# Neighborhood attention on one core: which queues issue the last stores of the output

## The chip, the core and the metric

The kernel runs on one core of a Trainium2 chip. The core has four engines that compute: TensorE (PE; its weight loads are shown apart as PEld), VectorE (DVE), ScalarE (ACT) and GpSimd (POOL). A fifth, SyncE (SP), issues transfers only. ACT and POOL can issue transfers too, each in the order of its own instructions. The metric is the device time of one execution in microseconds (us). A profile is one such execution with every instruction and transfer recorded; its span goes from the first instruction of the program to the last.

## What is computed

The reference is dilated 7x7 neighborhood attention with dilation 2 over an image of 224 x 224 pixels with 192 channels, one head, in bfloat16. Every pixel attends to 49 pixels, whose window is moved inwards at the image's edges:

```python
qkv = x @ wqkv                                  # 192 -> 3 * 192
r0 = clip(ir - half, 0, H - 1 - (ks - 1) * dil) # ks, dil = 7, 2
c0 = clip(ic - half, 0, W - 1 - (ks - 1) * dil)
kn, vn = the 49 rows of k and v that (r0, c0) + dil * (0..6) name
logits = einsum('bnc,bnkc->bnk', q, kn) * 192 ** -0.5
o = einsum('bnk,bnkc->bnc', softmax(logits), vn) @ wo
```

## The kernel before

**Tiling.** With dilation 2, rows of one parity only meet rows of the same parity, and columns likewise. The image is so cut into row classes `rc` (0 and 1) and column classes `cc` (0 and 1), with 112 rows and columns in each class. A step is 16 rows of one row class: 7 row tiles `ti` by 2 classes make `NSTEP` = 14 steps. A step holds `NSLOT` = 14 slots `s`, each of 16 rows by 8 columns of queries, that is 128 partitions, for both column classes. Slots are worked on in pairs, `J.m` = 0 to 6 with `ab` = 0 and 1, so that `s = 2 * J.m + ab`; the whole run has `NP` = 98 pairs, counted by `J.k`, and `J.n` is the step.

**Stages of a pair.** `stage1` multiplies queries and keys into `s` (L497) and takes the row maximum (L499, VectorE). `stage1b` is the exponential on ScalarE (L507). `stage2` transposes the probabilities on TensorE and copies them out of PSUM (L526, L527; L518 and L519 for the last pair). `stage3` multiplies them with the values into `o_ps` (L536); a column of ones beside the values gives the softmax's sum, whose reciprocal is taken in L542. `stage4` scales the output by it: on VectorE in L559, or, in the second slot of the last three pairs, with two instructions on ScalarE (L557), one for each column class. Those are slots 9, 11 and 13 of the last step.

**Stores.** The scaled slot is stored at the end of `stage4`. The 16 rows of a tile are not always evenly spaced in the image; `_aff_runs` cuts them into evenly spaced runs. In the last step (row class 1, row tile 6) the runs are 13 rows and three single rows. The 13 rows leave in one long store per slot (`put`, L565): 104 partitions, each with one contiguous piece of 768 B, 78 KB. All 13 of these, for slots 1 to 13, are issued by SP. The single rows are not stored slot by slot: the last step's outputs stand side by side in one tile, a reused `xs`, and `SHORT = {7: 1, NSLOT - 1: 8}` lets one short store carry one row for a group of slots (L576): at slot 7 three stores for slots 1 to 7 (8 partitions by 7 pieces, 42 KB), and at slot 13 three stores for slots 8 to 13 (8 by 6 pieces, 36 KB). The first three are issued by POOL at once. The last three are put on the list `end_q` and issued by ACT at the very end (L743 and L744).

Slot 0 has its own store code, because its columns wrap: many small pieces, queued in `pool_q` and issued by POOL (L588), some of them after each pair and the rest at the end (`pool_do`, L742).

**Order.** Each engine runs its instructions in the order in which the program wrote them (`in_order`, L745). A store waits in its issuer's queue for its data. All other waits are inserted by the framework from the tiles that are read and written; among them, a store takes one of a small number of semaphores in turn, and waits until that semaphore's last store has landed. After the last instruction each engine has a closing DRAIN and a barrier, which the profile puts under L771: SP waits there for all stores, and POOL gathers the other engines.

```python
                elif nj >= 8:
                    put(nc.sync)
...
                        if s < NSLOT - 1:
                            row(nc.gpsimd)
                        else:
                            end_q.append(row)
...
    pool_do(len(pool_q))
    for it in end_q:
        it(nc.scalar)
```

Of the kernel before, what the change touches and what calls it, by code (L numbers as in the profile page):

```python
# [21 lines left out]
NSLOT = 14  # L22
# [18 lines left out]
def _aff_runs(vals):  # L41
    out = []
    i, n = 0, len(vals)
    while i < n:
        j = i
        step = 1
        if i + 1 < n and vals[i + 1] > vals[i]:
            step = vals[i + 1] - vals[i]
            j = i + 1
            while j + 1 < n and vals[j + 1] - vals[j] == step:  # L50
                j += 1
        out.append((i, j - i + 1, vals[i], step))
        i = j + 1
    return out


def _rows(rc, ti):

    return [_phys(rc, 16 * ti + j) for j in range(16)]
# [7 lines left out]
def _win(t, p0, pn, off, dims):  # L67
    a = t[:]
    ps = a.ap[0][0]
    return bass.AP(a.tensor, a.offset + p0 * ps + off, [[ps, pn]] + [list(d) for d in dims])  # L70
# [18 lines left out]
def in_order(tc):  # L89

    last = {}
    for i in tc.nc.cur_bb.bb.instructions:
        if i.engine in last:
            tc.add_manual_dep(i, last[i.engine], mybir.DependencyInfo(mybir.DependencyClass.NoSync, mybir.DependencyReason.DATA), reason="program order")
        last[i.engine] = i.name
# [3 lines left out]
def kernel(  # L99
# [7 lines left out]
    nc = tc.nc  # L107
# [432 lines left out]
    def stage4a(J, ab):  # L540
        J.rs[ab] = stat.tile([128, 2], F32, name="rs", tag="rs")
        nc.vector.reciprocal(out=J.rs[ab][:], in_=J.o_ps[ab][:, C:C + 2])  # L542
        return J.rs[ab]

    def stage4(J, ab):
        rc, ti, s, o_ps = J.rc, J.ti, 2 * J.m + ab, J.o_ps[ab]
        rs = J.rs.get(ab) or stage4a(J, ab)
        if s > 0 and J.n == NSTEP - 1:

            o_sb = _win(XS[0], 0, 128, 2 * C * s, [[C, 2], [1, C]])  # L550
        elif s > 0:
            o_sb = work.tile([128, 2, C], BF, name="o_sb", tag="o_sb", bufs=6)
        else:
            o_sb = work.tile([128, 2, C], BF, name="o_s0", tag="o_s0")
        if J.k >= NP - 3 and ab == 1:
            for cc in range(2):
                nc.scalar.mul(o_sb[:, cc, :], o_ps[:, 194 * cc:194 * cc + C], rs[:, cc:cc + 1])  # L557
        else:
            nc.vector.tensor_tensor(out=o_sb[:], in0=_win(o_ps, 0, 128, 0, [[194, 2], [1, C]]),  # L559
                                    in1=rs[:].unsqueeze(2).to_broadcast([128, 2, C]), op=ALU.mult)  # L560
        prow = _rows(rc, ti)
        if s > 0:
            for (j0, nj, r0, rstep) in _aff_runs(prow):
                def put(eng, j0=j0, nj=nj, r0=r0, rstep=rstep):
                    eng.dma_start(out=op[r0: r0 + (nj - 1) * rstep + 1: rstep, 8 * s - 3:8 * s + 5, :],  # L565
                                  in_=o_sb[8 * j0:8 * (j0 + nj)].rearrange("p t c -> p (t c)"))

                if J.n < NSTEP - 1:
                    put(nc.gpsimd if nj < 8 and s % 2 == 1 else nc.sync)
                elif nj >= 8:  # L570
                    put(nc.sync)
                elif s in SHORT:

                    for j in range(nj):
                        def row(eng, p=8 * (j0 + j), r=r0 + j * rstep, a=SHORT[s]):
                            eng.dma_start(out=op[r, 8 * a - 3:8 * s + 5, :].rearrange("(t i) c -> i t c", i=8),  # L576
                                          in_=_win(XS[0], p, 8, 2 * C * a, [[2 * C, s + 1 - a], [1, 2 * C]]))
# [4 lines that stand above are left out]
            return  # L582
        for h in range(2):
            for (j0, nj, r0, rstep) in _aff_runs(prow[8 * h:8 * h + 8]):
                for (cc, i0, n, mem, pair) in ((0, 0, 3, 1, 0), (0, 3, 5, 0, 0), (1, 6, 2, 1, 3), (1, 0, 3, 1, 109), (1, 3, 3, 0, 109)):
                    p = 64 * h + 8 * j0 + i0 * nj
                    dst = op[r0: r0 + (nj - 1) * rstep + 1: rstep, pair:pair + n, mem * C:(mem + 1) * C]
                    pool_q.append(lambda dst=dst, p=p, m=n * nj, cc=cc: nc.gpsimd.dma_start(out=dst.rearrange("j i c -> i j c"), in_=o_sb[p:p + m, cc, :]))  # L588
# [17 lines left out]
    end_q = []  # L606
    SHORT = {7: 1, NSLOT - 1: 8}

    def pool_do(n):
        for _ in range(min(n, len(pool_q))):  # L610
            pool_q.pop(0)()
# [35 lines left out]
    for k in range(NP + 2):  # L647
# [22 lines left out]
        if k >= 2:  # L670
            stage3(pairs[k - 2], 0)
            stage3(pairs[k - 2], 1)
            if k >= NP:
                stage4a(pairs[k - 2], 0)
                stage4a(pairs[k - 2], 1)
            stage4(pairs[k - 2], 0)
            if k == NP - 1:
                stage4a(pairs[k - 2], 1)
# [6 lines left out]
        if k >= 2:  # L685
            stage4(pairs[k - 2], 1)
# [53 lines left out]
            g_row(1, 6, 1, 13, pool, last[1:])  # L740
        pool_do(4)
    pool_do(len(pool_q))  # L742
    for it in end_q:  # L743
        it(nc.scalar)  # L744
    in_order(tc)  # L745


# [28 lines left out]
```

## Time and profile before

| | |
|---|---|
| three runs, us | 365.96, 362.02, 364.18 (median 364.18) |
| profiled execution, us | 360.51 |
| its span, us | 358.7 |
| granted TensorE clock, mean | 0.995 |
| last step's long stores by SP (L565) | 13 of 78 KB, issue 794 to 873 ns |
| short stores by POOL (L576) | 3 of 42 KB, 593 to 620 ns |
| short stores by ACT (L576) | 3 of 36 KB, 301 to 538 ns |
| slot 0's stores by POOL (L588) | 150, 557 to 602 ns |

The profile's page gives for the whole span each engine's busy share, then the chain of work that ended last. Times of issue are those in which the issuing engine is held by the store; the transfer itself goes on after it. The transfers of the three issuers show as three queues, of which q1 and q10 are called hardware dynamic and q0 software dynamic:

```profile
q1 hardware_dynamic: 130052, 56.32, 78.5%
q0 software_dynamic: 5280, 1.71, 2.7%
q10 hardware_dynamic: 2120, 1.54, 2.3%
```

The columns are packets, MB, and the time of the packets as a share of 16 DMA engines over the span. POOL's stores are those of q0. The landing of a store is the moment at which its semaphore has its last update.

### The profile page before, as it was taken

The page shows a single profiled execution, that of the slowest core. Times are in us where ns is not written, and L with a number is a line of the kernel's source. Part 1 is how long each engine was busy: PE and PEld are TensorE (multiplying, and loading weights), DVE is VectorE, ACT ScalarE, POOL GpSimd, SP SyncE. Part 2 cuts the span into 40 slices and gives each one's busy share as a digit, 9 for nine tenths or more (in the row PEclk, how much of TensorE's full clock was granted, in tenths as well). Part 3 has the DMA queues.
Part 4 walks back from the last instruction along what each step waited for, and adds up shares of the span by engine and source line. Part 5 has one row for each costly group of instructions (what it writes and reads, how often), then busy time and mean ns, then how long its engine had stood idle before and what let it go on. Part 6 is the DMA issues. An engine that isn't in the chain of part 4 may idle for free.

```text
span 358.7 us, 19454 instructions
## 1 busy us (share of the span) xinstructions
PE 333.6 (93%) x8120; PEld 307.1 (86%) x8120; DVE 314.2 (88%) x744; ACT 308.2 (86%) x824; POOL 282.6 (79%) x445
## 2 busy tenths in 40 slices
PE   4788888998999999999999999999999999999872
PEld 2777777997999999999989999999999999999762
DVE  8967987897898998989989999899998989989893
ACT  6354777997999999999999999999999989999893
POOL 8966799999896996959969699596996878374182
PEclk9999999999999999999999999999999999999998
DMA  9999876799968979889898997999989965635423
GB/s 191 214 189 182 161 168 160 152 206 154 209 158 201 189 177 184 185 187 195 182 191 178 203 194 170 188 196 187 193 182 187 179 143 123 142 98 116 107 68 90
DMA packets 137539, 60.79 MB, mean 169 GB/s; under 512 B 88578, under 2 KB 136927, under 8 KB 137452
## 3 DMA queue, kind: packets, MB, share of 16 engines
q1 hardware_dynamic: 130052, 56.32, 78.5%
q0 software_dynamic: 5280, 1.71, 2.7%
q10 hardware_dynamic: 2120, 1.54, 2.3%
q8 instruction: 63, 1.03, 1.2%
q14 instruction: 24, 0.20, 0.2%
HBM read 0.29 MB, written 19.27 MB: 55 GB/s over the span
## 4 chain that ended last, share of the span: by engine, by line
PE 74%; DVE 10%; POOL 7%; ACT 5%; issue 2%; DMA 1%; DVEq 0%; SPq 0%; POOLq 0%; ACTq 0%
PE pv L341 17%; PE s L497 16%; PE o_ps L536 15%; PE pg L421 11%; PE pt_ps L526 10%; PE pgh L421 6%; ACT p L507 3%; POOL out_dram L588 2%; POOL xs L170 2%; DVE xb L160 2%; DVE nmx L499 2%; DVE g L329 1%; POOL xb L160 1%; POOL g L456 1%; ACT pt_sb L527 1%
## 5 line engine op out<-in xcount | busy, mean ns | idle before, releaser
L507 ACT ACTIVATE p<-s,nmx 128x224 bf16<-128x224 f32 x392 | 150.1, 450 | 25.7 <-DVE nmx L499 24.2
L499 DVE TENSOR_REDUCE nmx<-s 128x2 f32<-128x392 f32 (+1 forms) x196 | 102.5, 565 | 18.2 <-PE s L497 17.5
L456 POOL COPY g<-gx 64x512 bf16<-64x512 bf16 (+1 forms) x110 | 62.1, 564 | 52.7 <-ACT gx L331 45.8
L341 PE MATMUL pv<-wp,xs 128*64 128x192 bf16 x1624 | 93.1, 250 | 10.8 <-DVE xs L366 3.6
L341 PEld LDWEIGHTS <-xs 128*64 128x64 bf16 x1624 | 79.0, 112 | 24.0 <-issue 8.5
L559 DVE TENSOR_TENSOR o_sb<-o_ps,rs 128x384 bf16<-128x384 f32 x169 | 94.2, 558 | 5.9
L331 ACT CAST vf<-pv 128x384 bf16<-128x384 f32 x193 | 87.8, 522 | 11.1 <-PE pv L341 11.1
L588 POOL DMA_DIRECT2D out_dram<-o_s x150 | 84.6, 571 | 9.0 <-DVE rs L542 7.8
L536 PE MATMUL o_ps<-vd,pt_sb 128*64 128x193 bf16 x784 | 81.6, 246 | 2.3 <-ACT pt_sb L527 2.1
L497 PE MATMUL s<-xa,g 128*64 128x196 bf16 (+7 forms) x990 | 82.3, 233 | 1.2 <-ACT p L507 0.3
L497 PE MATMUL s<-xb,g 128*64 128x196 bf16 (+7 forms) x990 | 82.0, 232 | 0.7 <-DVE g L329 0.4
L536 PE MATMUL o_ps<-vf,pt_sb 128*64 128x193 bf16 x784 | 81.6, 246 | 0.0
L497 PEld LDWEIGHTS <-g 128*64 128x64 bf16 x1980 | 77.8, 110 | 3.6 <-issue 2.0
L536 PEld LDWEIGHTS <-pt_sb 128*64 128x64 bf16 x1568 | 71.5, 109 | 3.8 <-ACT pt_sb L527 3.2
L527 DVE COPY pt_sb<-pt_ps 128x1024 bf16<-128x1024 bf16 x92 | 63.2, 687 | 6.0 <-PE pt_ps L526 0.8
L526 PE MATMUL pt_ps<-ident,p 128*64 128x128 bf16 x1552 | 63.7, 219 | 0.0
L526 PEld LDWEIGHTS <-p 128*64 128x64 bf16 x1552 | 57.1, 110 | 4.9
L331 ACT CAST g<-pg 128x512 bf16<-128x512 f32 (+4 forms) x136 | 57.6, 470 | 2.3 <-PE pg L421 2.3
L421 PEld LDWEIGHTS <-aw 128*64 128x64 bf16 x1320 | 54.7, 110 | 3.9 <-issue 0.6
L421 PE MATMUL pg<-xb,aw 128*64 128x512 bf16 (+9 forms) x440 | 54.1, 269 | 0.0
L421 PE MATMUL pg<-xa,aw 128*64 128x512 bf16 (+9 forms) x440 | 52.3, 270 | 0.0
L170 POOL COPY xs<-xa 128x896 bf16<-128x896 bf16 x50 | 45.2, 930 | 1.4
(73 smaller groups left out, 283.9 us busy)
## 6 DMA issues: line engine op xcount, KB each, us to landing
vd<-vf SPq DMA_DIRECT2D x49, 336.9 KB
out_dram<-o_sb SPq DMA_DIRECT2D x156, 96.0 KB
out_dram<-o_s POOLq DMA_DIRECT2D x78, 9.0 KB, 3.9
out_dram<-o_sb SPq DMA_DIRECT2D x13, 78.0 KB
out_dram<-xs SPq DMA_DIRECT2D x13, 78.0 KB
vd<-vf SPq DMA_DIRECT2D x2, 337.8 KB
vd<-vf ACTq DMA_DIRECT2D x2, 336.9 KB
xa<-in_x_dram SPq DMA_TRANSPOSE x28
```

The costliest lines, as they stand in the source:

```text
L331: nc.scalar.copy(out=out_, in_=in_)
L341: nc.tensor.matmul(pv[64 * h:64 * h + 64, cc * C:(cc + 1) * C], lhsT=at(k, h), rhs=WP[(cc, pas)][:], start=(pas == 0), stop=(pas == 1))
L421: nc.tensor.matmul(o, lhsT=l, rhs=r, start=(pas == 0), stop=(pas == 1))
L456: nc.gpsimd.tensor_copy(out=G[rc][cc][p:p + 64, 1, s0:s0 + ns, :], in_=gx[p:p + 64, 0:ns * 128].rearrange("p (s q) -> p s q", q=128))
L497: nc.tensor.matmul(o, lhsT=w, rhs=r, start=(pas == 0), stop=(pas == 1))
L499: nc.vector.tensor_reduce(out=nmx[:], in_=_win(s_ps, 0, 128, lo, [[256, 2], [16, 14], [1, 16 - lo]]), axis=AX.XY, op=ALU.max, negate=True)
L507: nc.scalar.activation(out=J.p[:, ab, cc, :, z:z + 112].rearrange("p q (r k) -> p q r k", k=8), in_=_win(s_ps, 0, 128, cc * 256, [[8, 2], ...
L526: nc.tensor.transpose(pt_ps[64 * h:64 * h + 64, 4 * ab + 2 * cc + q, :], J.p[:, ab, cc, q, 64 * h:64 * h + 64], ident[:])
L527: (nc.scalar.copy if J.n == NSTEP - 1 and J.m < 5 else nc.vector.tensor_copy)(out=J.pt[:], in_=pt_ps[:])
L536: nc.tensor.matmul(o_ps[64 * h:64 * h + 64, cc * 193:cc * 193 + 193], lhsT=J.pt[:, 4 * ab + 2 * cc + q, 64 * h:64 * h + 64], rhs=V[h][:, ( ...
L559: nc.vector.tensor_tensor(out=o_sb[:], in0=_win(o_ps, 0, 128, 0, [[194, 2], [1, C]]), in1=rs[:].unsqueeze(2).to_broadcast([128, 2, C]), op ...
L588: pool_q.append(lambda dst=dst, p=p, m=n * nj, cc=cc: nc.gpsimd.dma_start(out=dst.rearrange("j i c -> i j c"), in_=o_sb[p:p + m, cc, :]))
```

## The change

The long stores of two slots of the last step get another issuer: slot 11 (`NSLOT - 3`) goes to POOL and slot 13 (`NSLOT - 1`) to ACT. The three short stores of the last group, which ACT issued one after the other, are dealt out to SP, POOL and ACT. In the order of instructions this gives: SP has 11 long stores in place of 13, and one short store behind them; POOL has, behind the last of slot 0's stores, the long store of slot 11 and one short store; ACT has, behind its last scaling, the long store of slot 13 and one short store in place of three. What is stored, and where, is the same.

```diff
                 if J.n < NSTEP - 1:
                     put(nc.gpsimd if nj < 8 and s % 2 == 1 else nc.sync)
                 elif nj >= 8:
-                    put(nc.sync)
+
+                    put({NSLOT - 3: nc.gpsimd, NSLOT - 1: nc.scalar}.get(s, nc.sync))
                 elif s in SHORT:
...
     pool_do(len(pool_q))
-    for it in end_q:
-        it(nc.scalar)
+    for i, it in enumerate(end_q):
+        it((nc.sync, nc.gpsimd, nc.scalar)[i % 3])
     in_order(tc)
```

## The prediction

> **What bounds the kernel now.** I read the page first, then the last 6 us engine by engine, since the change touches only stores behind the last computation.
>
> ```profile
> span 358.7 us, 19454 instructions
> PE 333.6 (93%) x8120; PEld 307.1 (86%) x8120; DVE 314.2 (88%) x744; ACT 308.2 (86%) x824; POOL 282.6 (79%) x445
> PE 74%; DVE 10%; POOL 7%; ACT 5%; issue 2%; DMA 1%; DVEq 0%; SPq 0%; POOLq 0%; ACTq 0%
> ```
>
> Over the whole span TensorE sets the pace, and the edit leaves all of that as it is. The chain of waits, printed for its last stretch, ends like this (start, length, what):
>
> ```profile
> 353.33 0.03 ACTq L576
> 353.36 0.28 ACT xs L557
> ```
>
> The chain closes at 353.64 with ScalarE's last scaling, yet the span ends at 358.74: 5.1 us (1.4% of the span) hold only stores, their landings and the closing barrier. No edit of stores can gain more than a part of that. The timeline of those microseconds, each row asked for in a narrow window (start, length):
>
> ```profile
> 352.63 0.80 SPq L565 DMA_DIRECT2D out_dram<-xs  x1
> 353.52 0.81 SPq L565 DMA_DIRECT2D out_dram<-xs  x1
> 354.43 0.79 SPq L565 DMA_DIRECT2D out_dram<-xs  x1
> 355.32 0.81 SPq L565 DMA_DIRECT2D out_dram<-xs  x1
> ...
> 352.48 0.41 ACT L557 ACTIVATE xs<-o_ps,rs 128x192 bf16<-128x192 f32 x1
> 353.22 0.41 ACT L557 ACTIVATE xs<-o_ps,rs 128x192 bf16<-128x192 f32 x1
> 353.66 0.54 ACTq L576 DMA_DIRECT2D out_dram<-xs  x1
> 354.24 0.30 ACTq L576 DMA_DIRECT2D out_dram<-xs  x1
> 354.58 0.46 ACTq L576 DMA_DIRECT2D out_dram<-xs  x1
> ...
> 351.78 0.57 POOL L588 DMA_DIRECT2D out_dram<-o_s  x1
> ```
>
> SP's four rows are the long stores of slots 10, 11, 12 and 13, one every 0.90 us. Slot 11's data is ready at 352.90 and slot 13's at 353.64 (the ends of L557), but they are issued at 353.52 and 355.32. So slot 13 waits 1.68 us for its turn in SP's queue. Its landing is the last one: the semaphore records have it at 357.66, 2.34 us after its issue began, and SP's closing waits end on it (us in total, times, longest):
>
> ```profile
> SPq L771 <- DMA out_dram<-xs: 1.2, 2, 0.7
> ```
>
> From that landing to the span's end it is 1.08 us of semaphore steps. The last view is of the closing line, L771 (op, count, duration in ns min/median/max, first and last start):
>
> ```profile
> L771 SPq EVENT_SEMAPHORE  x12: 17/28/28, 356.2 to 358.7; - x12
> L771 POOLq EVENT_SEMAPHORE  x4: 17/17/17, 358.0 to 358.6; - x4
> L771 POOLq DRAIN  x3: 40/93/5003, 351.4 to 358.5; - x3
> L771 ACTq DRAIN  x2: 8/124/239, 355.1 to 358.2; - x2
> ```
>
> The reader is to see the 5003. POOL ends with a DRAIN that begins beside its last store (351.44), ends at 356.44, and stands ahead of the barrier step at 358.02 in which POOL gathers the other engines. Before the change it is covered for 1.58 us. The change gives POOL two later stores.
>
> **The change, part by part.** Nothing before 352.9 us moves: SP keeps its stores up to slot 10, POOL its list, and the computation does not depend on these stores.
>
> SP loses the long stores of slots 11 and 13 and gains one short store. Slot 12 (data ready at 353.32, the end of VectorE's last L559) takes slot 11's place at 353.52; the short store follows one pitch later, 354.42, and lasts 0.30 to 0.54 by ACT's rows, so SP is done at 354.87 instead of 356.13. By ACT's rows (issue starts 353.66, 354.24, 354.58; landings recorded at 355.77, 356.36, 356.87) a short store lands 2.1 to 2.3 us after its issue begins: 356.5 to 356.7.
>
> ACT swaps three short stores for the long one of slot 13 and one short. It is free at 353.66 as now. The long one costs ACT something between its own short rows (0.54) and SP's long rows (0.81); I take 0.81, being the same transfer. Short one at 354.51 to 354.97, landing at 356.8. ACT's three short issues ended at 355.04, so behind it ACT's drain (0.24) comes no later. The added wait on slot 13's data is on ACT's own work; nothing else is queued there.
>
> POOL gains the long store of slot 11 and a short one, behind its last L588 (free at 352.36). Slot 11 waits for ACT's 352.90 and starts at 352.95; the short one waits for ACT's 353.64 and starts at 353.69. The nearest rows of POOL are its 42 KB stores, L576 (0.62 a piece, landing after 2.6 to 2.7); the far one is the seven early L565 stores, up to 0.73 and landing after 2.9 to 5.3 while the DMA engines were nine tenths busy. In the last stretch they are about half busy, so I take L576: issue ends at 353.6 and 354.31, landings at 355.6 and 356.35. Behind these two waits on ACT stands nothing in POOL's queue but its drain, for which the closing barrier waits.
>
> Stores alone: the last landing goes from 357.66 to 356.8, a gain of 0.86 us. On this the Trainium skill speaks against the change: its page "DMA: Bandwidth & Descriptors", section "Issuing engines are not separate DMA queues", says that transfers from all issuers interleave on the same 16 DMA engines, and that issuing from several saves only issue time, usually small beside the transfer. The trace has issue at 0.90 us a store beside 1.5 us from issue's end to landing, so small is not the word here; by the page alone the term would be near zero.
>
> Now the drain. What ends it the trace does not say, so it is bounded by three anchors. After the end of POOL's last issue (352.36) it lasted 4.08 us: with the last issue ending at 354.31, that is 358.39. After the landing of that store (353.88) it lasted 2.56: 356.35 + 2.56 = 358.91. After its own start, which lay beside the last store, 5.00: 353.6 + 5.0 = 358.6. I take the middle, 358.6. POOL then gathers at 358.64, and the 0.73 from there to the end are as before (358.02 to 358.74): the span ends near 359.4, 0.6 us later than now. Lower bound: the drain follows nothing POOL issues, and the end is 356.8 + 1.08 = 357.9, a gain of 0.9. Upper bound: the short store lands after 5.3 us (359.0) and the drain 2.56 behind it (361.55), span end 362.3, a loss of 3.6.
>
> On the drain the skill's page "VectorE: DVE Perf Modes", section "The DRAIN you can't avoid", has boilerplate drains at about 12 ns on all engines; the row says 5003 ns on POOL behind its stores and 8 to 239 on ACT, so the trace disagrees for POOL. By the page the lower bound would be the result.
>
> **Rivals.**
> Forecast: POOL's drain takes the place of SP's queue, +0.4 to +0.9 us. For it: the drain is long only where POOL has just issued stores (5003 ns, against 40 and 93 in the two that follow). Against it: one instance only. Chance 0.55.
> Gain as written: the drain stays covered and the last landing sets the end, 357.9, gain 0.9 us. For it: nothing shows what the drain waits for. Chance 0.27.
> Shared engines: three issuers' packets mix, and the last landing stays near 357.6, about 0. Against it: the DMA engines' share between 354 and 357 is 0.53, 0.58 and 0.51, so there is room. Chance 0.08.
> Slower: the drain is POOL working off runs of its stores. The last six stores have 3 x 56 + 6 + 9 + 9 = 192 contiguous runs, begun at 348.80 and drained at 356.44, 40 ns a run; the two new ones have 13 x 8 + 6 x 8 = 152, 6.1 us more: drained at 362.5, the end at 363.3, a loss of 4.6 us (1.3%). It decides once a run costs over 10 ns, for 152 x 10 ns uses up the 1.58 us of cover. Against it: those stores had landed by 353.9, and copies of POOL that stand right behind bursts of stores earlier in the run took their usual 0.6 us. Chance 0.10.
> That the stores are not moved is no rival: the instruction order of the two kernels differs in exactly these rows on SP, ACT and POOL.
>
> **How the numbers follow.** The profiled execution took 360.51 us (span 358.74 and 1.77 around it); the median of the three runs is 364.18, and they spread over 3.9 us. The forecast gives 361.1 on the former, a ratio of 1.0017, so 364.8 on the median; the gain case gives 363.3, shared engines 364.2, the slower case 368.8. A median of three such runs wanders by some 1.3 us, so about 1.7 is added on either side: 361.6 from the gain case, 366.5 from the forecast, to which I add 0.5 for the late landings of the upper bound. Range 361.7 to 367.0; the slower case stays outside. About 1% (3.6 us) is what a measurement of this kernel can tell from no change. The forecast and the two small cases lie within it save for that wander (a few per cent on either side), and the slower case is mostly beyond: faster 0.04, same 0.84, slower 0.12.
>
> **What would show it.** SP's last issue near 354.4 with a short store, ACT's long store at 353.66, POOL's two at 352.95 and 353.69, and the last landing near 356.8: then the stores went as costed. POOL's DRAIN ending at 358.4 to 358.9, later than SP's last closing wait, and the span near 359.4: then the forecast holds. A drain ending before 357.2 makes it wrong towards the gain; one ending after 360 means that it grows with what POOL stores.

## The result, and the profile after

The changed kernel took 365.33 us (median of 10 runs, 362.55 to 366.71); the kernel before took 361.83 us (median of 10, 360.37 to 365.96). The ratio is 1.0059, 95% interval 1.0031 to 1.0087: slower, by less than 1%. The two medians alone would give 1.0097. Ratios leave out runs more than 1.5% above the fastest of their kernel (one of twelve and four of six in two of the experiments below). The profiled execution took 363.49 us, with this span:

```profile
span 361.7 us, 19456 instructions
```

Two different things stand in the 3.0 us between the two spans, and the first step is to part them. ScalarE's last scaling ended at 353.63 before and at 355.80 after. Up to there both kernels run the same instructions, and the distance between the two traces does not grow steadily: it comes in two jumps, 1.06 us near 224 us and 1.30 us near 268 us. This is the wait view of the changed kernel from 266 to 280 us (us in total, times, longest):

```profile
ACT vf L331 <- DMA vd<-vf: 1.6, 1, 1.6
DVE nmx L499 <- PE s L497: 1.3, 2, 1.1
```

ScalarE may not write new values into `vf` before an earlier copy out of it has landed. In this execution the copy was late; in the same stretch of the kernel before the first row is absent. The chain of waits has such a copy ahead of the first jump too, from 217.94 to 223.04. Nothing that was moved runs there.

The second thing is the end. From the last scaling to the end of the span it took 5.11 us before and 5.91 us after: 0.80 us more. The timeline after, in the order SP, ACT, POOL (start, length):

```profile
354.80 0.80 SPq L565 DMA_DIRECT2D out_dram<-xs  x1
355.69 0.81 SPq L565 DMA_DIRECT2D out_dram<-xs  x1
356.60 0.43 SPq L577 DMA_DIRECT2D out_dram<-xs  x1
...
355.39 0.41 ACT L557 ACTIVATE xs<-o_ps,rs 128x192 bf16<-128x192 f32 x1
355.83 1.51 ACTq L565 DMA_DIRECT2D out_dram<-xs  x1
357.44 0.32 ACTq L577 DMA_DIRECT2D out_dram<-xs  x1
...
355.36 0.59 POOL L565 DMA_DIRECT2D out_dram<-xs  x1 [0.85 <-ACT xs L557]
356.12 0.57 POOL L577 DMA_DIRECT2D out_dram<-xs  x1 [0.17 <-issue]
```

SP is done earlier, as meant: its last issue ends 1.22 us behind the last scaling, against 2.50 before. ACT's long store holds it for 1.51 us, where SP's take 0.80. The closing line and SP's waits:

```profile
L772 SPq EVENT_SEMAPHORE  x12: 17/28/28, 357.1 to 361.6; - x12
L772 POOLq EVENT_SEMAPHORE  x4: 17/17/17, 361.0 to 361.6; - x4
L772 POOLq DRAIN  x3: 40/93/4837, 356.1 to 361.4; - x3
L772 ACTq DRAIN  x2: 8/122/237, 357.8 to 361.2; - x2
```

```profile
SPq L772 <- DMA out_dram<-xs: 1.9, 3, 1.0
SPq L772 <- PEq L772: 1.9, 2, 1.4
```

POOL's long DRAIN begins at 356.10 and takes 4837 ns, so it ends at 360.94; POOL's first closing step stands at 361.0 right behind it. SP has had its last landing (3.56 us behind the last scaling) and its last drain by 359.69, and then waits 1.4 us more for the barrier; the name PE in that row is only the one whose signal the profile saw last. Before, the order was the other way round: POOL's drain was over 1.58 us ahead of the barrier step.

### The profile page after: what moved, and what is told of

The parts are those of the page before. It is cut to its first block, busy times and chain, and to the rows that moved or that the text cites. A ratio compares the mean times of both kernels' runs of the same rounds, so it can differ in the third digit from the quotient of the medians.

```text
span 361.7 us, 19456 instructions
## 1 busy us (share of the span) xinstructions
PE 333.2 (92%) x8120; PEld 306.7 (85%) x8120; DVE 314.4 (87%) x744; ACT 308.3 (85%) x824; POOL 282.9 (78%) x447
## 3 DMA queue, kind: packets, MB, share of 16 engines
q8 instruction: 63, 1.03, 1.2%
## 4 chain that ended last, share of the span: by engine, by line
PE 68%; DVE 10%; ACT 7%; POOL 7%; DMA 4%; issue 2%; DVEq 0%; POOLq 0%; ACTq 0%
PE pv L341 16%; PE s L497 15%; PE o_ps L536 14%; PE pg L421 10%; PE pt_ps L526 9%; PE pgh L421 5%; ACT p L507 5%; DMA vd<-vf 3%; DVE nmx L499 2%; POOL out_dram L589 2%; POOL xs L170 2%; DVE xb L160 2%; POOL xb L160 1%; DMA out_dram<-o_sb 1%; POOL g L456 1%
```

## The experiments

All of them are read by one clock, us behind the end of ScalarE's last scaling, since what comes ahead of that point differs from execution to execution in kernels that are equal there: it ended between 353.63 and 359.34 in the ten executions up to `pool_many`. Each number of this table comes from the instruction and semaphore records of one profiled execution. Five of the kernels ran once only, so their times are not compared: `pool_long_only` 361.29, `pool_short_only` 366.99, `late_copy` 368.21, `early35_sp` 388.60 and `late20_sp` 370.15 us.

| kernel | POOL's last store or copy ends | DRAIN ends | DRAIN behind it | last landing | end of span |
|---|---|---|---|---|---|
| before | -1.28 | 2.81 | 4.08 | 4.03 | 5.11 |
| same_as_before | -1.28 | 2.81 | 4.08 | 3.99 | 5.07 |
| after | 0.89 | 5.13 | 4.25 | 3.56 | 5.91 |
| after_again | 0.89 | 5.14 | 4.25 | 3.55 | 5.92 |
| slot10_pool | -0.14 | 4.02 | 4.17 | 3.75 | 4.89 |
| no_pool | -1.29 | 2.79 | 4.08 | 3.99 | 4.95 |
| pool_long_only | 0.15 | 4.32 | 4.17 | 3.93 | 5.10 |
| pool_short_only | 0.93 | 5.09 | 4.16 | 3.98 | 5.88 |
| late_copy | 2.54 | 6.64 | 4.10 | 3.99 | 7.42 |
| pool_many | 2.59 | 7.08 | 4.49 | 4.40 | 7.86 |
| early35_sp | -0.24 | 1.73 | 1.97 | 4.05 | 5.42 |
| late20_sp | -1.28 | 1.32 | 2.60 | 3.97 | 5.31 |
| slot0_sp | -1.45 | 0.87 | 2.33 | 4.00 | 5.15 |
| slot0_sp_after | 0.89 | 3.97 | 3.08 | 3.63 | 4.79 |

The theory: POOL's closing DRAIN follows POOL's last store and now ends last. Rivals: the moved stores cost time in the middle too; the drain grows with the runs that POOL stores; the drain does not depend on the stores at all.

**Two yardsticks.** `same_as_before` walks over a copy of the list and is otherwise the kernel before; `after_again` is the changed kernel.

> The kernel before under another name, as the yardstick of what two equal programs differ by. Both theories: ratio 1.000 within about 0.3%, and 5.1 us from the end of ScalarE's last scaling to the end of the span (5.11 in the profile before).

> The changed kernel once more. Theory 1, only the end of the run is different: 5.9 us from ScalarE's last scaling to the end (5.9 in the profile after, 5.1 before), so a ratio near 1.002, and the 2.2 us by which the scaling ended later in the profile after were chance (two stalls in the middle, near 224 and 268 us). Rival, the moved stores cost something in the middle too: ratio near 1.006 again, and the last scaling ends 1 us or more later than in the two profiles of the kernel before.

Measured: 0.9996 (0.9971 to 1.0022) for the one, 1.0013 (0.9986 to 1.0039) for the other, 12 runs each beside 35 of the kernel before. The end takes 5.92 us, within 0.01 of the first time, and the last scaling ended at 354.17, beside 353.63 and 354.38 in the two executions of the kernel before. So the end is what differs, and the 2.2 us in the middle did not come back. 0.80 us is 0.22% of the run, which lies in the second interval and below the first.

**One store of POOL at a time.** First the long store of slot 11 alone, then one short store alone:

```diff
-                    put(nc.sync)
+                    put({NSLOT - 3: nc.gpsimd}.get(s, nc.sync))
```

> The kernel before with slot 11's long store by POOL, nothing else moved. POOL's issue ends 0.1 us before ScalarE's last scaling does. If the drain follows POOL's last store: it ends 4.0 to 4.1 us behind the scaling, and the end takes 4.8 to 4.9 us, 0.2 to 0.3 less than before. If the drain costs time per contiguous run of the stores (40 ns each): 104 runs are 4.2 us more work, 8 us or more to the end.

```diff
-    for it in end_q:
-        it(nc.scalar)
+    for i, it in enumerate(end_q):
+        it((nc.scalar, nc.gpsimd, nc.scalar)[i % 3])
```

> The kernel before with one of the three last short stores by POOL, nothing else moved. SP's thirteen long stores are as before, so without POOL's drain the end takes 5.1 us. If the drain follows the last store: its issue ends 0.7 us behind the last scaling, the drain 4.8 to 4.9 behind it, and the end takes 5.6 to 5.7 us.

The short store alone gives the whole loss: 5.88 us, with SP's last landing at 3.98 as before. This is the closing drain of that kernel, 359.7 being 0.32 behind its last scaling:

```profile
L771 POOLq DRAIN  x3: 40/102/4778, 359.7 to 364.9; - x3
```

The long store alone, the 104 runs, is nearly free: 5.10 us. The drain is so no matter of runs (8 us or more was the price). It missed the 4.8 to 4.9 expected from the drain for two reasons that the records show. POOL began the store 0.30 us behind ScalarE's data, where 0.05 had been taken. And SP's slot 13, issued 0.89 us earlier than before, landed only 0.10 earlier: from issue to landing it took 3.13 us in place of 2.34. That second part is what the rival of shared engines would give; it stands on one execution, and the cause was not isolated.

**Does the drain wait for the store?** POOL gets a copy behind its last store that waits for ScalarE's last scaling; no store is moved, and the copy adds to no output.

```diff
     pool_do(len(pool_q))
+    pool(out=VD[0][:, 0:7, 0:2 * C], in_=_win(XS[0], 0, 128, 2 * C * 7, [[2 * C, 7], [1, 2 * C]]))
     for it in end_q:
```

> The kernel before with no store moved; POOL copies 128 x 2688 elements of the last outputs to a tile no longer used, behind its last store and behind ScalarE's last scaling (some 2.5 us), and so its DRAIN begins later than its last store. The copy adds to no output. If the drain waits for something of the last store (4.1 us behind its issue): it is over when the copy ends, and the end takes 5.1 us as before. If it is a piece of work of its own length, 4 to 5 us from when POOL gets to it: it ends 6.5 us or more behind the scaling, and the end takes 7.3 us or more.

POOL's timeline and its closing line in that kernel:

```profile
355.99 1.74 POOL L588 DMA_DIRECT2D out_dram<-o_s  x3
359.14 2.42 POOL L743 COPY vd<-xs 128x2688 bf16<-128x2688 bf16 x1 [1.42 <-ACT xs L557]
...
L772 POOLq DRAIN  x3: 40/102/6533, 359.1 to 366.2; - x3
```

The stores were issued by 357.73, and the copy ran to 361.56. The drain began beside the copy, at 359.13, and took 6533 ns, to 365.66: 4.10 us behind the end of the copy, 7.93 behind the last store. Had it waited for something of the store, it would have been over 0.3 us after the copy. So it follows POOL's last instruction, be it a store or a copy, and takes some 4 us of its own in this kernel. The forecast had the right length but tied it to the store. (In every run POOL issues stores, 25 at the least, so what the drain would take on a POOL without stores is not shown.)

**Five stores by POOL.** The long stores of slots 11 and 13 and the three short ones:

```diff
-                    put(nc.sync)
+                    put({NSLOT - 3: nc.gpsimd, NSLOT - 1: nc.gpsimd}.get(s, nc.sync))
...
+        it((nc.gpsimd, nc.gpsimd, nc.gpsimd)[i % 3])
```

> The kernel before with five of its last stores by POOL: the long ones of slots 11 and 13 and the three short ones, 352 contiguous runs. Issue at about 0.6 us each ends 2.4 us behind the last scaling. If the drain follows the last store at 4.1 to 4.3 us: the end takes 7.4 us, 2.3 more than before, ratio 1.006. If it grows with the runs or the number of stores, it takes longer than that behind the last issue: with 40 ns a run, 14 us more.

Ratio 1.0126 (1.0075 to 1.0178), with the end at 7.86 us. The 2.75 us more at the end are 0.76%, just inside that interval; the 1.006 expected is below it. The drain grew by 0.41 us over the kernel before for five stores; with one store it was 0.09 and 0.08, with two 0.17. That is 0.08 a store and far from 40 ns a run, which would be 14 us.

**Without POOL, and with POOL early.** In the first slot 13's long store goes to ACT and the short stores to SP, ACT and ACT, and slot 11's long store stays with SP; in the second slot 10's long store, whose data is ready 1.03 us ahead of the last scaling, is the only one moved.

```diff
-                    put(nc.sync)
+                    put({NSLOT - 1: nc.scalar}.get(s, nc.sync))
...
+        it((nc.sync, nc.scalar, nc.scalar)[i % 3])
```

> The change without POOL: the long store of slot 13 by ACT, slot 11's by SP as before, the three short ones by SP, ACT and ACT. POOL's drain is covered again by every theory. If SP and ACT issue independently (long store 0.8 us on ACT): last landing 3.6 us behind the last scaling, 4.9 us to the end. If the two share what makes their transfers (ACT's long store took 1.51 us beside SP's in the profile after): 5.1 to 5.3 us, no gain.

```diff
-                    put(nc.sync)
+                    put({NSLOT - 4: nc.gpsimd}.get(s, nc.sync))
```

> The kernel before with one edit: the long store of slot 10 is issued by POOL, all others as before. If POOL's closing DRAIN follows its last store (4.1 to 4.25 us behind the end of that issue in the two profiles), that issue ends 0.4 us before ScalarE's last scaling does, the drain ends 3.8 us behind the scaling, SP's last landing 3.5 behind it, and the whole end takes 4.65 us: 0.45 less than before, ratio 0.999. If a late store of POOL costs more than it saves in any case: over 5.1 us.

`no_pool`: ratio 1.0016 (0.9980 to 1.0051). ACT's rows there:

```profile
356.83 1.51 ACTq L565 DMA_DIRECT2D out_dram<-xs  x1
358.44 0.66 ACTq L576 DMA_DIRECT2D out_dram<-xs  x2
```

The long store holds ACT for 1.51 us again, and the last landing is at 3.99, no earlier than in `same_as_before`. That speaks for a shared resource: 416 + 144 = 560 runs are issued by SP and ACT in 3.3 to 3.5 us whichever of them issues (from slot 10's store on). ACT's short stores point the same way: one took 0.54 us beside a long store of SP (before, 353.66) and 0.32 us when SP was through (after, 357.44). The end at 4.95 is near the 4.9 of the other forecast and 0.12 below `same_as_before`, but not through an earlier landing: SP is through its closing waits sooner (4.13 for 4.25). It takes these waits one by one at 0.06 us each, and after the store that lands last one of them follows here, three in `same_as_before`. What is shared was not isolated: ACT's long store was never issued with SP idle.

`slot10_pool`: ratio 0.9992 (0.9967 to 1.0016). The end is 0.2 us shorter than in the two executions of the kernel before (4.89), not 0.45. SP's last landing came at 3.75, not 3.5, and SP was through its waits at 4.07. POOL's start is again 0.30 late, and the drain ends at 4.02, just ahead of that. It is the shortest end of those that leave the middle as it is, and too small a gain for the runs to show.

**What the drain works at.** Since it grew by 0.08 us a store, four kernels take stores from POOL: those of slot 0 in the first three steps, in the two steps before the last, and in all but the last step, the last also in the changed kernel.

```diff
-                    pool_q.append(lambda dst=dst, p=p, m=n * nj, cc=cc: nc.gpsimd.dma_start(out=dst.rearrange("j i c -> i j c"), in_=o_sb[p:p + m, cc, :]))
+                    pool_q.append(lambda dst=dst, p=p, m=n * nj, cc=cc, eng=nc.sync if J.n < 3 else nc.gpsimd: eng.dma_start(out=dst.rearrange("j i c -> i j c"), in_=o_sb[p:p + m, cc, :]))
```

> The kernel before with the 35 stores of slot 0 of the first three steps issued by SP: POOL issues 125 stores in place of 160. So far the closing DRAIN took 4.08, 4.17, 4.16, 4.25 and 4.49 us behind POOL's last issue with 160, 161, 161, 162 and 165 stores, and 4.10 behind a copy. Theory 1, it works through all stores of POOL's run at 0.08 us each: 1.2 us behind the last issue. Theory 2, only the stores since some earlier point late in the run count (some 49): 4.08 again. Theory 3, a fixed piece of work: 4.08 again. The end takes 5.1 us in all three.

> The kernel before with the 20 stores of slot 0 of the two steps before the last issued by SP: POOL issues 140 stores. Theories 1 and 2 (0.08 us a store): the drain takes 2.4 us behind POOL's last issue. Theory 3, a fixed piece of work with little for each store: about 4.08. The end takes 5.1 us in all three.

> The kernel before with all stores of slot 0 by SP except those of the last step: POOL issues 25 stores. Theories 1 and 2: the drain takes at most 2.1 us. Theory 3: about 4.1. The end takes 5.1 us; the ratio is 1.00 if SP's queue has room in the middle of the run, more if stores and loads wait there for the 135 that are added.

> The changed kernel with the same move: POOL issues 27 stores. Theories 1 and 2: the drain ends 0.89 + 2.25 = 3.1 us behind ScalarE's last scaling, is covered by the last landing at 3.55, and the end takes 4.65 us, 0.45 less than in the kernel before. Theory 3: the end takes 5.8 us as in the changed kernel.

No theory holds. Only `late20_sp` comes near a price of the first two (2.60 us for 2.4); `early35_sp` came at 1.97 for 1.2 or 4.08. A fixed piece of work falls: 1.97 and 2.60 us are well below 4.08. The number of POOL's stores falls as the only measure: 125 stores give 1.97, 25 give 2.33, 27 give 3.08. What sets the length is open; near the 160 stores of this kernel it is 4.1 us and 0.08 more for each. (The ends of the first two, 5.42 and 5.31, are above the 5.1 expected. Their drains were long over; SP was through its waits 0.2 us later. In `late20_sp` seven of SP's waits follow the store that lands last, where three do in the kernel before; in `early35_sp` the cause is open.)

But the pair answers the question of the change. Where the drain is short, the same edit gains at the end: 4.79 against 5.15 us. The two closing drains:

```profile
L771 POOLq DRAIN  x3: 40/93/3254, 429.7 to 437.0; - x3
```

```profile
L772 POOLq DRAIN  x3: 40/102/3672, 439.4 to 443.6; - x3
```

The first is that of `slot0_sp`, the second of `slot0_sp_after`, where it ends 3.97 behind the scaling, level with SP's last wait (3.96). This gain of 0.36 us is read from one execution of each, and whole runs don't show it: the medians of six runs are 445.44 and 445.45 us. As kernels both are of no use, at ratios of 1.2077 (1.2019 to 1.2134) and 1.2248 (1.2200 to 1.2296). The wait view of `slot0_sp` over the whole span points to the reason:

```profile
POOL g L456 <- ACT gx L331: 187.2, 47, 11.9
DVE nmx L499 <- PE s L497: 59.9, 48, 5.9
ACT vf L331 <- DMA vd<-vf: 43.4, 10, 6.5
```

The 135 small stores hold SP for 0.66 us or more each, 111 us in all. The copies of values stand behind them in SP's queue: the one issued at 99.71, for which ScalarE waited 6.2 us, had seven of these stores ahead of it since 88.2. ScalarE waits 43.4 us in all for such copies. (The first row is POOL's idle time, which costs nothing by itself.)

## Why the prediction was right

**The mechanism was right.** Forecast was that POOL's drain takes the place of SP's queue as the last thing, at +0.4 to +0.9 us. It did, at +0.80. `pool_short_only` shows that POOL's last store alone makes the loss, and `slot0_sp_after` that the edit gains at the end once the drain is short.

**That the time came so close is luck.** 365.33 lies in the range, 0.5 us from the 364.8 forecast. But the base of the forecast was 364.18, the median of three runs, and ten runs gave 361.83; from there the forecast's 0.6 us would have been 362.4. The two medians differ by 3.50 us, of which the end explains 0.80. The range also held the gain as written (363.3) and shared engines (364.2), so the time could not tell these from the forecast. The records of the end do.

**The anchors.** The profile after does not tell the three apart: the drain ended 4.25 us behind POOL's last issue (4.08 before), 2.43 behind the landing of that store (2.56) and 4.84 behind its own start (5.00). That start lay 0.35 us ahead of the last store before the change, not beside it. `late_copy` decides: the landing was long past, from its own start the drain took 6.53, and only the end of POOL's last instruction fits, at 4.10. The middle anchor, which the forecast took, was so the wrong one. It put the end at 5.73 us behind the last scaling, 0.21 later than the anchor that holds, and so made up for part of what the terms below left out.

**Terms that were mis-sized.** POOL's short store was costed from 0.05 us behind ScalarE's data; it began 0.32 behind. With the drain's 0.17 of growth that is 0.44 more, less 0.05 for a shorter issue: by the first anchor the end would have been 5.52, and it came at 5.91. ACT's long store was taken at 0.81 from SP's rows and held ACT for 1.51; so the last landing gained 0.47 us and not 0.86. Here the rule of the Trainium skill ("DMA: Bandwidth & Descriptors", section "Issuing engines are not separate DMA queues"), that transfers from several issuers interleave and only issue time is spared, would have put the gain near zero: the 0.47 measured lies between it and the sum's 0.86, and `no_pool`, with SP and ACT alone, got no earlier landing than `same_as_before`. The skill's 12 ns for a boilerplate drain ("VectorE: DVE Perf Modes", section "The DRAIN you can't avoid") would have made the edit a gain, if the page means this drain too; POOL's 4837 ns decide against it.

**Rivals.** The gain as written is out for this kernel: the drain was not covered. Working off runs at 40 ns is out: 152 more runs made the drain 0.17 us longer. Shared engines are borne out in part, by ACT's 1.51 us and the landings that came no earlier, but were not what ended last.

**What stays open.** The first comparison's 0.59% is more than the end's 0.22%. The repeat had 0.13%. The intervals meet between 1.0031 and 1.0039. No trace shows a cause outside the end that belongs to the change, and ScalarE's waits on `vd<-vf` differ by more than the gap among executions whose code is equal up to the last stores (none before, 1.6 us in `same_as_before`, 6.1 in `pool_short_only`); whether anything beyond the 0.80 us belongs to the change is not settled.

## What to carry to other kernels

Before giving the last transfers to an engine that is free, look at what that engine still has to do after them: here its closing drain of 4 us was covered by 1.58 us, and a store that came 2.2 us later used that up. Issue on a second queue is not issue for nothing: read what the second issuer pays while the first is issuing. And when a gain is expected in the last microseconds, count from the last computation, since what precedes it can differ by more than the edit is worth: here by up to 5.7 us in executions of code that is equal there.

## What the runs showed of the hardware

- POOL's closing DRAIN took 1.97 to 4.49 us behind POOL's last instruction in the 14 profiled executions, while ACT's two took 8 and 237 ns after the change; behind a copy it was 4.10.
- From slot 8 of the last step on, a long store of 104 runs held SP for 0.79 to 0.81 us in all 14 executions (up to 0.94 in the slots before), and ACT, beside SP, for 1.51 in the four executions in which ACT issued one.
- In the last stretch POOL began a store 0.29 to 0.35 us behind its data from ScalarE or VectorE; SP 0.03 behind VectorE's, ACT 0.03 behind its own.
- From the start of issue to landing the long stores of slots 10 to 13 took 2.0 to 3.1 us, on POOL's queue (2.03 to 2.65) no longer than on SP's (2.26 to 3.13).
